# HGRN2 recurrence with a max-out feed-forward: five early steps of a hand-written order moved, and span 2's keys loaded ahead of its queries

## The chip, the cores and the metric

The kernel runs on one core of a Trainium2 chip. The metric is the device time of one launch in microseconds (us), lower is better. A core has TensorE (PE; its weight loads are listed apart as PEld), VectorE (DVE), ScalarE (ACT), GpSimd (POOL) and SyncE (SP, which here only issues transfers, its queue shown as SPq). Each engine works through its own list of instructions strictly in order and waits for others by semaphores; 16 DMA engines move data between HBM and the on-chip SBUF; matmul results lie in eight PSUM banks.

## The reference, cut to what matters

```python
# q, k, v, f_logit: (4, 8, 768, 48) = batch, heads, sequence, head size
f = 1.0 / (1.0 + np.exp(-f_logit))
for t in range(S):
    state = f[:, :, t, :, None] * state + np.einsum('bhd,bhe->bhde', k[:, :, t], v[:, :, t])
    y[:, :, t] = np.einsum('bhd,bhde->bhe', q[:, :, t], state)
x = y.transpose(0, 2, 1, 3).reshape(3072, 384)
return np.maximum(x @ w1, x @ w2) @ w_out          # w1, w2: 384 x 1024, w_out: 1024 x 384
```

## The kernel before

The 3072 tokens are cut into 12 spans of 256 tokens; span s belongs to batch s % 4, and the recurrence is carried from span s to span s + 4. Two neighbouring tokens share a partition (even and odd), so a span is 128 partitions; it is worked as two chunks of 64 partitions. Decays become products within a chunk: q and k are scaled by exponentials of summed log gates, the intra-chunk part is a masked matrix of q against k, and the state is added through further matmuls. The feed-forward uses max(a, b) = b + relu(a - b): the kernel forms wd = w1 - w2 and m2 = w2 @ w_out once, and each span then costs relu(x @ wd) @ w_out + x @ m2.

Nothing is scheduled by a compiler. One long string, ORDER, lists every step; a word is a step's letter, the span (or the quarter of a weight), an engine letter (a ScalarE, v and w VectorE, p GpSimd, s SyncE) and, after @, a PSUM bank or, for loads, an SBUF slot. The last loop of the kernel runs the words one by one, so the string is at the same time the order of each engine's instruction list. Of it, these words matter here:

| word | what it is | line |
|---|---|---|
| Lf, Lk, Lq, Lv | load gates, keys, queries, values of a span into one slot (SP's queue) | 115 |
| Wa, Wb, Wo | load halves of w1, w2, w_out into two slots each (SP's queue) | 126, 130 |
| E, F, G | gate = exp(-f), ell = ln(1 + gate), one = exp(-ell of the odd token) (ScalarE) | 192, 196, 200 |
| e | e = ell even + ell odd, what the sum over tokens is taken of | 203 |
| C | that sum, on TensorE | 207, 210 |
| X, Z | exponentials of the sum, for keys (inv) and for queries and decays (dec) (ScalarE) | 217, 222 |
| i, j | multiply the even half of the keys by `one`; of the queries by (1 + gate) | 226, 230 |
| K, Q | the scaled keys and queries in bf16 | 237, 240 |
| V | values to bf16 | 104 |
| t, u | transposes of keys and of queries on TensorE | 257 |
| U | both transposes copied out of PSUM (trs) | 104 |
| A, m | queries against keys on TensorE; that, masked, to SBUF (at_m) | 274, 282 |
| S, z, y | a span's output: its first state part on TensorE, a one-column VectorE copy from it (look), the rest | 314, 330, 342 |
| D, n | the sum that updates the state; its addition on VectorE | 358, 375 or 377 |
| Y | the span's output to bf16 (xT) | 104 |
| d, r | x @ wd on TensorE; relu to SBUF (gT) | 398, 407 or 409 |
| o, oz, b | the output products; their copy to SBUF | 424, 104 |
| ws | a quarter of wd = w1 - w2 | 485 |
| wc, wt, wx | w2 to bf16, transposed on TensorE, copied out of PSUM (ob) | 104, 459, 104 |
| wo | a quarter of w_out to bf16 | 104 |
| wm, wn | m2 on TensorE; its copy to SBUF (m) | 475, 104 |

Steps copy through one helper, so many operations carry its line, 104. Keys and queries are loaded as float32 into slots that the weights used before; i and j write in place over them, and K and Q read them after that. TensorE's list around the change runs, in words: the d of spans 0 and 1, wm0, wm2, C2, wm1, C3, o0.0, oz0.0, t2, D2, u2, o1.0, A2.0, A2.1, o0.1, S2 (with D3 mixed in), D3, t3, y2, u3, o1.1.

The step that the change reorders around:

```python
def step_i(s, e):
    even = loaded[s]["k"][:, :, 0, :]
    engines[e].tensor_mul(even, even, one[s])

def step_j(s, e):
    even = loaded[s]["q"][:, :, 0, :]
    engines[e].scalar_tensor_tensor(out=even, in0=gate[s][:, :, 1, :], scalar=1.0, in1=even,
                                    op0=ALU.add, op1=ALU.mult)
```

Of the kernel before, what the change touches and what calls it, by code (L numbers as in the profile page):

```python
# [21 lines left out]
t0@0 Lv1s@13 u0@0 E1 D0@2 Wb0s U0v@0 F1 n0.0v A0.0@0 e1p G1 Wa0s n0.1v S0@4 Wb1s A0.1@2 z0 Wa1s i1p  # L22
m0.0v@0 C1@6 Wo0s Z1 Wo1s j1v X1 V1a K1v Lf2s@16 Q1v t1@6 wc0a m0.1v@2 u1@6 D1@0 wc1a U1v@6 y0 n1.0v
n1.1v A1.0@6 Y0a@4 N1.1w S1@2 ws0p m1.0v@6 A1.1@0 wt0@4 z1 m1.1v@0 wt1@5 Lf3s@17 ws1p wx0a@4 d0.0@6
wx1a@5 y1 wc3v d0.1@7 wc2v Y1v@2 wt2@5 r0.0a@6 wt3@4 ws2v d1.0@2 Lq2s@0 ws3p d1.1@3 wx2v@5 d1.2@6
Lk2s@1 wx3v@4 d0.2@0 r1.0v@2 wo2a wo3p d0.3@1 Lv2s@2 wo0a wo1p d1.3@7 r0.1v@0 E2 wm0@2 Lk3s@8 F2
r1.1v@6 wm2@3 E3 e2p Lq3s@16 G2 C2@6 F3 j2v wm1@7 Lv3s@17 wn2a@3 e3v X2 C3@3 Z2 i2v o0.0@0 wn0a@2
Lf4s@9 K2v wn1a@7 V2a Q2v oz0.0@0 t2@6 Lf5s@1 X3 D2@4 N0.1v G3 u2@6 n2.0v o1.0@2 b0.0a@0 i3p U2v@6
Lk4s@0 n2.1v j3v A2.0@6 Lq5s@2 b1.0a@2 A2.1@4 K3p o0.1@0 m2.0v@6 Z3 V3a Lv4s@10 m2.1v@4 S2@6 E4 D3@2
z2 Q3v Lq4s@8 t3@4 F4 y2 u3@4 G4 e4p Lk5s@16 o1.1@1 b0.1a@0 U3v@4 Y2a@6 i4p E5 n3.0v Lf7s@9 n3.1v  # L30
C4@0 b1.1v@1 d2.0@4 X4 Z4 A3.0@2 K4p Lv5s@1 A3.1@6 F5 d2.1@5 m3.0v@2 G5 d2.2@0 Lk7s@17 r2.0a@4
m3.1v@6 e5p S3@2 d2.3@1 V4a z3 C5@4 j4v Lq7s@0 y3 X5 Q4v Z5 t4@6 Y3a@2 D4@4 r2.1v@0 N2.1p Lf6s@10
u4@6 i5p d3.0@2 n4.0v d3.2@0 U4v@6 Lf8s@8 d3.1@3 j5v d3.3@1 r3.0a@2 N4.0w Lk6s@11 N3.1p o2.0@6 n4.1v
# [514 lines left out]
```

## Time and profile before

| | |
|---|---|
| time, median of 3 runs | 139.65 us (139.54 to 139.70) |
| the profiled execution: own time, span from first to last instruction | 139.23 us, 137.4 us |
| busy: PE, DVE, ACT, POOL | 120.9, 104.0, 81.2, 43.9 us |
| granted TensorE clock | 1.00 |
| traffic | 28.68 MB, loads of spans in pieces of 384 bytes, DMA engines busy nine tenths or more up to about 93 us |

The page of the profile gives each engine's busy time, then the waits, then a chain: from the last instruction back to what released it, and so on to the start. A line of the timeline is start, duration, engine, line, operation, output <- input, how many instructions are merged, and in brackets the idle time just before it and what ended that. Because the lists are in order, an engine's instruction can be late by its own inputs or by whatever stands ahead of it.

### The profile page before, as it was taken

What the parts mean: (1) busy time and instruction counts of PE and PEld (TensorE: products, weight loads), DVE (VectorE), ACT (ScalarE), POOL (GpSimd) and SP (SyncE); (2) the same over time, 40 slices, a digit from 0 to 9 for tenths busy, and PEclk for the clock granted to TensorE, in tenths of its full rate; (3) what the DMA queues carried; (4) which work ended last, traced back from release to release, by engine and by line L of the source; (5) the groups of instructions that cost most, each with busy time, mean ns of one, the idle gap of its engine ahead of it and who ended that gap; (6) DMA issues with size and microseconds to landing.
All of it is one profiled execution on the core that took longest, in us unless ns stands there. A gap on an engine that the chain in (4) does not pass through costs nothing.

```text
span 137.4 us, 5777 instructions
## 1 busy us (share of the span) xinstructions
PE 120.9 (88%) x2575; PEld 89.9 (65%) x2575; DVE 104.0 (76%) x165; ACT 81.2 (59%) x120; POOL 43.9 (32%) x53
## 2 busy tenths in 40 slices
PE   0047397999998999999999999999999999999991
PEld 0035285775656688666787667886578876778671
DVE  5778999995897799888969995988988369620321
ACT  3646564269945982888499454988817570226210
POOL 7704109542160786217104320002804912000000
PEclk9999999999999999999999999999999999999999
DMA  4999999999999999999999999994104001103033
GB/s 108 270 261 261 367 389 378 347 257 262 268 263 244 246 272 252 241 256 293 277 235 319 336 278 255 328 284 99 46 0 176 1 7 62 34 28 119 0 114 115
DMA packets 55193, 28.68 MB, mean 209 GB/s; under 512 B 50304, under 2 KB 52736, under 8 KB 55168
## 3 DMA queue, kind: packets, MB, share of 16 engines
q1 hardware_dynamic: 55024, 28.25, 78.6%
q8 instruction: 20, 0.33, 1.0%
q10 hardware_dynamic: 144, 0.07, 0.2%
q14 instruction: 5, 0.04, 0.1%
HBM read 23.59 MB, written 4.72 MB: 206 GB/s over the span
## 4 chain that ended last, share of the span: by engine, by line
PE 72%; DMA 13%; DVE 5%; SPq 3%; ACT 3%; issue 1%
PE banks L424 30%; PE banks L398 20%; DMA slots<-in_moe_w_out_dram 10%; PE banks L342 5%; PE banks L257 4%; PE banks L274 4%; PE banks L475 3%; PE banks L314 3%; DMA slots<-in_f_logit_dram 3%; SPq L126 2%; PE banks L358 2%; PE banks L207 2%; DVE at_m L282 2%; ACT wo L104 1%; DVE slots L230 1%
## 5 line engine op out<-in xcount | busy, mean ns | idle before, releaser
L424 PE MATMUL banks<-wo,gT 128*128 128x384 bf16 (+2 forms) x200 | 35.3, 320 | 0.0
L398 PE MATMUL banks<-xT,wd 128*128 128x256 bf16 x288 | 34.1, 273 | 1.2 <-POOL wd L485 0.9
L398 PEld LDWEIGHTS <-wd 128*128 128x128 bf16 x288 | 27.0, 98 | 5.3 <-POOL wd L485 1.0
L282 DVE TENSOR_TENSOR at_m<-banks,mask 128x1024 bf16<-128x1024 f32 x24 | 28.8, 1217 | 2.2 <-PE banks L274 2.0
L424 PEld LDWEIGHTS <-gT 128*128 128x128 bf16 x200 | 19.2, 98 | 11.9
L407 ACT ACTIVATE gT<-banks 128x1024 bf16<-128x1024 f32 x15 | 15.2, 1019 | 11.4 <-PE banks L398 10.6
L203 POOL TENSOR_TENSOR e<-ell 128x384 bf16<-128x384 f32 x9 | 9.1, 1019 | 26.9 <-ACT ell L196 21.4
L424 PE MATMUL banks<-m,xT 128*128 128x384 bf16 (+2 forms) x75 | 15.9, 321 | 0.0
L409 DVE TENSOR_SCALAR gT<-banks 128x1024 bf16<-128x1024 f32 x9 | 10.9, 1219 | 6.3 <-PE banks L398 6.3
L104 DVE COPY trs<-banks 128x2048 bf16<-128x2048 bf16 x10 | 12.0, 1220 | 4.6 <-PE banks L257 4.6
L104 ACT COPY ob<-banks 128x384 f32<-128x384 f32 (+2 forms) x15 | 7.5, 506 | 13.2 <-PE banks L424 12.6
L104 ACT CAST xT<-banks 128x768 bf16<-128x768 f32 x10 | 8.0, 800 | 9.0 <-PE banks L342 8.9
L104 DVE COPY ob<-banks 128x384 f32<-128x384 f32 (+2 forms) x14 | 7.2, 541 | 7.5 <-PE banks L424 5.6
L192 ACT ACTIVATE gate<-slots 128x768 f32<-128x768 f32 x12 | 10.0, 837 | 4.4 <-DMA slots<-in_f_logit_dram 4.4
L342 PE MATMUL banks<-at_m,vb 64*64 64x128 bf16 x576 | 11.5, 224 | 0.0
L380 POOL TENSOR_TENSOR st<-tmp_s,dec 128x192 bf16<-128x192 f32 x8 | 4.1, 510 | 20.7 <-PE banks L274 12.9
L274 PE MATMUL banks<-trs 48*64 48x128 bf16 x384 | 9.9, 230 | 0.8 <-DVE trs L104 0.8
L226 POOL TENSOR_TENSOR slots<-slots,one 128x384 f32<-128x384 f32 x7 | 8.1, 1160 | 7.5 <-ACT one L200 6.9
L196 ACT ACTIVATE ell<-gate 128x768 f32<-128x768 f32 x12 | 10.1, 843 | 0.5
L207 PE MATMUL banks<-e,u_inc 128*128 128x384 bf16 x12 | 4.2, 353 | 6.9 <-DVE e L203 6.7
L342 PEld LDWEIGHTS <-vb 64*64 64x64 bf16 x576 | 10.0, 111 | 0.0
L240 DVE TENSOR_TENSOR qp<-slots,dec 128x768 bf16<-128x768 f32 x10 | 9.4, 951 | 0.1
(64 smaller groups left out, 173.2 us busy)
## 6 DMA issues: line engine op xcount, KB each, us to landing
slots<-in_f_logit_dram SPq DMA_DIRECT2D x12, 384.0 KB, 6.3
slots<-in_k_dram SPq DMA_DIRECT2D x12, 384.0 KB, 6.0
slots<-in_q_dram SPq DMA_DIRECT2D x12, 384.0 KB, 6.2
slots<-in_v_dram SPq DMA_DIRECT2D x12, 384.0 KB, 6.0
slots<-in_moe_w_dram SPq DMA_DIRECT2D x4, 768.0 KB, 9.2
out_dram<-ob SPq DMA_DIRECT2D x7, 384.0 KB, 5.4
out_dram<-ob SPq DMA_DIRECT2D x9, 192.0 KB, 1.9
slots<-in_moe_w_out_dram SPq DMA_DIRECT2D x2, 768.0 KB, 13.5
```

The costliest lines, as they stand in the source:

```text
L104: (nc.scalar.copy if e == "a" else engines[e].tensor_copy)(out, in_)
L192: nc.scalar.activation(flat(gate[s]), flat(loaded[s]["f"]), AF.Exp, bias=0.0, scale=-1.0)
L196: nc.scalar.activation(flat(ell[s]), flat(gate[s]), AF.Ln, bias=1.0, scale=1.0)
L203: engines[e].tensor_add(pad("e", s)[:, :, 0:D], ell[s][:, :, 0, :], ell[s][:, :, 1, :])
L240: engines[e].tensor_mul(pad("qp", s)[:, :, :, 0:D], by_parity(loaded[s]["q"]), both(dec[s][:, 0:HD].rearrange("p (h d) -> p h d", h=H)))
L274: nc.tensor.matmul(out=ps[h * HC:(h + 1) * HC, j % 2, par, :], lhsT=t[rows, h, 0, j, par, :], rhs=t[rows, h, 1, j].rearrange("p a t -> p ( ...
L282: nc.vector.tensor_mul(at[s][:, jj].rearrange("p r j a t -> p (r j) (a t)"), banks[:, b:b + 2, :].rearrange("p r (j x) -> p (r j) x", j=2) ...
L342: nc.tensor.matmul(out=ys[s][h][cols, kt, :], lhsT=window(vb[rows, par], head, off), rhs=m[rows, head // 4, head % 2, head // 2 % 2, par, ...
L398: nc.tensor.matmul(out=ps[:, f, :], lhsT=wd[:, kt, ff * C:(ff + 1) * C], rhs=x_flat(g)[:, kt, :], start=(kt == 0), stop=(kt == KT - 1))
L407: nc.scalar.activation(dst, src, AF.Relu)
L409: nc.vector.tensor_relu(dst, src)
L424: nc.tensor.matmul(out=ps, lhsT=x, rhs=w, start=(n == 0), stop=(n == KT + FG - 1))
```

## The change

Only the string ORDER differs. On the engines this means:

- Y1 goes from VectorE to ScalarE, ws3 and e2 from GpSimd to VectorE, wo1 from GpSimd to ScalarE, and wo0 with it stands ahead of wo2 on ScalarE.
- j3 (queries of span 3, VectorE) stands behind the two m2 and z2 rather than ahead of them.
- On SP's queue the keys of span 2 are loaded ahead of its queries, and the two loads swap slots 0 and 1.
- On VectorE i2 (keys of span 2) comes ahead of j2 (queries of span 2), and both ahead of e3. The list was j2, e3, i2, K2, Q2; it becomes e2, i2, j2, e3, K2, Q2.

TensorE's list is unchanged.

```diff
-wx1a@5 y1 wc3v d0.1@7 wc2v Y1v@2 wt2@5 r0.0a@6 wt3@4 ws2v d1.0@2 Lq2s@0 ws3p d1.1@3 wx2v@5 d1.2@6
-Lk2s@1 wx3v@4 d0.2@0 r1.0v@2 wo2a wo3p d0.3@1 Lv2s@2 wo0a wo1p d1.3@7 r0.1v@0 E2 wm0@2 Lk3s@8 F2
-r1.1v@6 wm2@3 E3 e2p Lq3s@16 G2 C2@6 F3 j2v wm1@7 Lv3s@17 wn2a@3 e3v X2 C3@3 Z2 i2v o0.0@0 wn0a@2
+wx1a@5 y1 wc3v d0.1@7 wc2v Y1a@2 wt2@5 r0.0a@6 wt3@4 ws2v d1.0@2 Lk2s@0 ws3v d1.1@3 wx2v@5 d1.2@6
+Lq2s@1 wx3v@4 d0.2@0 r1.0v@2 wo0a wo1a wo2a wo3p d0.3@1 Lv2s@2 d1.3@7 r0.1v@0 E2 wm0@2 Lk3s@8 F2
+r1.1v@6 wm2@3 E3 e2v Lq3s@16 G2 C2@6 F3 i2v j2v wm1@7 Lv3s@17 wn2a@3 e3v X2 C3@3 Z2 o0.0@0 wn0a@2
...
-Lk4s@0 n2.1v j3v A2.0@6 Lq5s@2 b1.0a@2 A2.1@4 K3p o0.1@0 m2.0v@6 Z3 V3a Lv4s@10 m2.1v@4 S2@6 E4 D3@2
-z2 Q3v Lq4s@8 t3@4 F4 y2 u3@4 G4 e4p Lk5s@16 o1.1@1 b0.1a@0 U3v@4 Y2a@6 i4p E5 n3.0v Lf7s@9 n3.1v
+Lk4s@0 n2.1v A2.0@6 Lq5s@2 b1.0a@2 A2.1@4 K3p o0.1@0 m2.0v@6 Z3 V3a Lv4s@10 m2.1v@4 S2@6 E4 D3@2 z2
+j3v Q3v Lq4s@8 t3@4 F4 y2 u3@4 G4 e4p Lk5s@16 o1.1@1 b0.1a@0 U3v@4 Y2a@6 i4p E5 n3.0v Lf7s@9 n3.1v
```

## The prediction

> **What bounds the kernel now.** I read the page first (busy times), then the chain of waits in order of time, then the timelines of VectorE, TensorE and GpSimd around the change, and last the table of transfers. The page:
>
> ```profile
> PE 120.9 (88%) x2575; PEld 89.9 (65%) x2575; DVE 104.0 (76%) x165; ACT 81.2 (59%) x120; POOL 43.9 (32%) x53
> DMA  4999999999999999999999999994104001103033
> ```
>
> TensorE does most, but an average does not say where it waits. The chain does:
>
> ```profile
> 14.37 14.11 DMA slots<-in_moe_w_out_dram
> 28.47 0.02 issue
> 28.50 1.57 ACT wo L104 x2
> 30.07 0.04 issue
> 30.11 2.76 PE banks L475 x16
> ...
> 37.35 0.35 DVE st L377
> 37.70 0.04 issue
> 37.74 1.23 DVE trs L104
> 38.97 0.26 DVE tmp_s L375
> 39.23 1.35 DVE slots L230
> 40.58 2.28 DVE at_m L282 x2
> 42.86 0.04 issue
> 42.90 0.41 PE banks L257 x16
> ```
>
> Up to 30.11 the second half of w_out bounds; up to 37.3 TensorE; then VectorE, with j3 (L230) in the middle, until t3 at 42.90. From there to 134.67 the chain holds TensorE alone, without a gap. So whatever t3 or u3, the next steps that wait for VectorE, win or lose arrives at the end undiminished; nothing can be lost or won later unless a new wait appears.
>
> VectorE's list, where the change swaps i2 and j2 (lines 226 and 230):
>
> ```profile
> 32.93 0.56 DVE L230 SCALAR_TENSOR_TENSOR slots<-gate,slots 128x384 f32<-128x384 f32 x1 [1.35 <-DMA slots<-in_k_dram]
> 33.60 0.56 DVE L203 TENSOR_TENSOR e<-ell 128x384 bf16<-128x384 f32 x1
> 34.15 0.56 DVE L226 TENSOR_TENSOR slots<-slots,one 128x384 f32<-128x384 f32 x1
> ```
>
> j2 sat idle for a load. The two loads, issued at 24.60 (q2) and 28.22 (k2):
>
> ```profile
> slots<-in_q_dram SPq DMA_DIRECT2D x1, 384.0 KB, 8.1
> slots<-in_k_dram SPq DMA_DIRECT2D x1, 384.0 KB, 5.9
> ```
>
> So q2 landed at 24.60 + 8.1 = 32.7 and k2 at 28.22 + 5.9 = 34.1. The bracket names keys, but j2 needs q2 and ran while k2 was under way; both transfers are on one queue, 1.4 us apart, and DMA is full. e3 stands behind j2 and ahead of i2, so today it needs only the first of the two loads. TensorE took C3, which needs e3, without a pause, at 34.37.
>
> **The change, part by part.**
>
> *Ahead of C3: gains.* ws3 leaves GpSimd. There ws3 (24.36 to 26.17) ran beside VectorE's ws2 (24.87, 2.12 us long; a product of the same size takes 0.95 at line 240). On VectorE the two run one after the other from about 24.3, when the last half of w1 is in: 24.3 + 2 x 0.95 = 26.2. d1.2, which waited 0.31 for ws2, then starts at the end of d1.1, 26.73. Y1 on ScalarE costs 0.80 in a stretch where ScalarE idles (2.31 ahead of 24.79) and frees 0.95 of VectorE. wo0 and wo1 go ahead of wo2 on ScalarE: their half landed at 13.48 + 12.8 = 26.3, so they run (2 x 0.8) before the other half lands at 28.47, and m2's product loses its 0.28 wait. Together TensorE reaches C2 and wm1 0.31 + 0.28 = 0.59 earlier; e2 on VectorE, after F2 (30.84 + 0.84), ends at 32.25 and costs C2 at most 0.1. TensorE would be ready for C3 at 34.37 - 0.59 + 0.08 = 33.86. Without ScalarE's spare time, wo1 would cost E2 0.8; with f2 landing at 29.9 the cover holds.
>
> *At C3: a loss.* The queue's places keep their times: I take 32.7 for k2 and 34.1 for q2, because f2, f3, q2 and k2 land 1.3 to 1.5 us apart with full engines and nothing ahead of them in SP's queue changes. SP does not gain or lose either: slots 0 and 1 are free at 23.87 (ws1), before it gets there. VectorE: i2 waits for G2 (32.32 + 0.51), runs 32.9 to 33.5; j2 waits for q2, 34.17 to 34.73; **e3 now stands behind both**, 34.72 to 35.28; C3 at 35.33 instead of 34.37, a shift of 0.96, with TensorE idle for 35.33 - 33.86 = 1.47. The start after a landing is the free term: before, j2 started 0.2 after it with two semaphore instructions ahead; now one wait is left, 0.04 taken, so the shift is 0.85 to 1.12. The 0.59 won ahead is swallowed by this wait. K2 (35.3 to 36.25) and Q2 (to 37.1) end before t2 and u2 come, at 36.52 + 0.96 and 37.22 + 0.96. Values of span 2 land at 35.5 as before. The load into slot 1 (f5) waits for Q2, 37.1 instead of 36.85; its landing is 7 us after issue with the queue full, so I cost it at nothing; a gap in the queue would cost 0.3 and would first show at F5.
>
> *From C3 to t3: a part comes back.* u2 38.18, o1.0 38.52, A2.0 39.45 + 0.96 = 40.41; U2 is done by then (38.64 + 1.23 = 39.87). With j3 gone, m2.0 starts at 40.41 + 0.47 (the distance of A3.0 and m3.0, 47.35 to 47.82) = 40.88 and the second m ends at 43.23. TensorE reaches t3 at 42.52 + 0.96 = 43.48 and finds it free: t3's wait of 0.38 is gone. Net at t3: 0.96 - 0.38 = +0.58.
>
> *At u3: a part goes again.* j3 is now between z2 and Q3, and Q3 releases u3:
>
> ```profile
> 42.77 0.14 DVE L330 COPY look<-banks 128x1 f32<-128x1 f32 x1
> 42.84 0.94 DVE L240 TENSOR_TENSOR qp<-slots,dec 128x768 bf16<-128x768 f32 x1
> ...
> 44.20 0.41 PE L257 MATMUL banks<-ident,qp 64*128 64x64 bf16 x16
> ```
>
> z2 needs S2. S2 starts at 41.92 + 0.96 = 42.88, is done 0.40 later (41.92 to 42.27, and 0.05); then z2 to j3 0.07, j3 0.56 (GpSimd idle beside it; 1.44 before, when K3 ran there), 0.10 as between j4 and Q4, Q3 0.94, 0.05 to TensorE: 2.12 in all, u3 at 45.00. TensorE's own path from S2 to u3 is 0.60 + 1.30 = 1.90. So u3 waits 0.22 (0 to 0.35, as S2's end is modelled).
>
> *Sum:* 0.96 - 0.38 + 0.22 = +0.80 (0.45 to 1.10). The profiled execution goes from 139.23 to 140.03, its span from 137.4 to 138.2. The runs' median stands 0.42 above that execution; 139.65 + 0.80 = 140.45.
>
> **Rivals.** About 0.2% (0.28 us) is what a measurement of this kernel can tell from no change.
>
> 1. *VectorE's order bounds, not the load: no slower.* If q2 lands by 33.45, i2, j2 and e3 run back to back from G2: e3 ends at 32.87 + 3 x 0.56 = 34.55, C3 at 34.60, shift 0.23; u3 0.23 - 0.38 + 0.22 = +0.07, that is 139.72. It decides below a landing of 33.6, where the sum falls under 0.28. Against it: the second load of this pair landed at 34.1. Chance 0.07.
> 2. *The loads run ahead: faster.* If the whole queue gained over 1.1 us (f3, k2, q2), e3 would no longer bind; with 1.4, C3 at 33.9, shift -0.47, u3 -0.63: 139.0. For it: the engines moved 374 GB/s in the stretch of the weights against 252 from 28.47 on. Against it: their pieces differ, and those do not change. Chance 0.05.
> 3. *Q3 meets e4 on GpSimd.* Q3 is due at 43.99, e4 starts at 44.40, when F4 is done, by a load that does not move:
>
> ```profile
> 39.15 1.44 DVE L230 SCALAR_TENSOR_TENSOR slots<-gate,slots 128x384 f32<-128x384 f32 x1
> ...
> 44.40 1.00 POOL L203 TENSOR_TENSOR e<-ell 128x384 bf16<-128x384 f32 x1 [4.23 <-ACT ell L196]
> ```
>
> j3 beside K3 (38.36 to 40.17) ended 0.42 after K3, ws2 0.82 after ws3: a VectorE product that starts second stands until GpSimd is through. If Q3 came 0.41 later than I have it, it would end at 45.40 + 0.82, u3 at 46.27, +2.07: 141.7. In its time it is first, and GpSimd waits instead, as i4 (51.18, 1.81 long) beside Q4. [...] Chance 0.05.
> 4. *TensorE goes slow in the idle 1.47.* Sixteen transposes took 0.61 at 16.69 and 0.41 at 36.52, so the array was slower early on, though the granted clock is shown as 1.00 throughout; the longest pause since is 0.88, ahead of 22.15, and the six products behind it took 0.83 like those at 23.92. A pause of 1.47 has no row. If it brought back the early rate for the 4.6 us from 15.83 to 20.43, that would cost up to 4.6 x (1 - 0.41 / 0.61) = 1.5 more: 141.95. [...] Chance 0.03.
>
> **How the numbers follow.** The forecast has 0.80; its own range, 140.1 to 140.75, with 0.1 for the spread of runs is 140.0 to 140.85. With rival 1 (139.72) taken in at the lower end and 0.1 for Q3 a little late at the upper, 139.7 to 140.95 leaves out rivals 2, 3 and 4, 0.13. Slower: 0.80 + 0.05 + 0.03 = 0.88; same 0.07; faster 0.05.
>
> **What would show it.** Right: VectorE runs i2 at about 32.9, j2 idles until 34.1 to 34.2, e3 ends near 35.3, TensorE has a gap of about 1.5 before line 207 there; the chain holds the q2 load, j2 and e3; no wait before t3, a short one before u3 released by Q3 (line 240); then TensorE without gaps, everything 0.8 later. Wrong: C3 without a gap, q2 landing before 33.6, or a gap before u3 over 1 us.

## The result, and the profile after

The changed kernel takes 141.50 us (median of 4 runs, 141.42 to 141.65) against 139.68 (139.54 to 140.08) for the kernel before: ratio 1.0128, 95% interval 1.0101 to 1.0155. Slower, as forecast, but 1.8 us slower and not 0.8, and outside the range given. A second measurement of the same kernel (changed_again below) gave 141.18 against 140.00, ratio 1.0099 (1.0065 to 1.0132). The profiled execution of the kernel before took 139.23, 0.45 less than the median of its runs here, so shifts that are read against that profile come out about that much larger than the 1.8 between the medians.

The page of the changed kernel, the counterpart of the first two lines shown of before:

```profile
PE 121.1 (87%) x2575; PEld 89.9 (64%) x2575; DVE 104.1 (75%) x166; ACT 83.0 (59%) x122; POOL 40.4 (29%) x50
DMA  4999999999999999999999699994104001013033
```

As before, busy shares tell nothing: TensorE does the same work in a longer span. The chain of waits in order of time (start, duration, what), from the load of the queries on:

```profile
28.36 5.99 DMA slots<-in_q_dram
34.34 0.02 issue
34.37 0.04 DVE slots L230
34.40 0.44 issue
34.84 0.56 DVE e L203
35.41 0.05 issue
35.45 0.34 PE banks L207
...
43.41 0.16 DVE look L330
43.57 0.48 DVE slots L230
...
44.14 1.64 DVE qp L240
45.78 0.05 issue
45.82 0.41 PE banks L257 x16
...
53.62 0.36 PE banks L358 x29
53.97 0.66 issue
54.63 0.21 PE banks L358 x3
...
129.79 7.19 PE banks L424 x55
```

The first group is the loss that was forecast: the load of q2, then j2 (L230), then e3 (L203), then C3. The second is z2 (L330), j3 and a Q3 (L240) of 1.64, where 0.94 was forecast, then u3. The third is a pause of TensorE inside D4. Everything after that keeps its lateness to the last 55 matmuls: 129.79, against 127.48 before. VectorE's list at the first group, TensorE's C3 and u3 with the idle time before each, and the two loads, issued at 24.74 (keys) and 28.36 (queries):

```profile
33.21 0.56 DVE L226 TENSOR_TENSOR slots<-slots,one 128x384 f32<-128x384 f32 x1 [0.87 <-DMA slots<-in_q_dram]
34.37 0.56 DVE L230 SCALAR_TENSOR_TENSOR slots<-gate,slots 128x384 f32<-128x384 f32 x1 [0.60 <-DMA slots<-in_q_dram]
34.84 0.55 DVE L203 TENSOR_TENSOR e<-ell 128x384 bf16<-128x384 f32 x1
```

```profile
35.45 0.34 PE L207 MATMUL banks<-e,u_inc 128*128 128x384 bf16 x1 [1.33 <-DVE e L203]
...
45.82 0.41 PE L257 MATMUL banks<-ident,qp 64*128 64x64 bf16 x16 [0.91 <-DVE qp L240]
```

```profile
slots<-in_k_dram SPq DMA_DIRECT2D x1, 384.0 KB, 8.3
slots<-in_q_dram SPq DMA_DIRECT2D x1, 384.0 KB, 6.0
```

Keys landed at 24.74 + 8.3 = 33.0, queries at 28.36 + 6.0 = 34.4. The bracket of i2 names the queries, but i2 reads keys and started 0.2 after they were in; queries were still 1.2 away. So i2 and j2 each wait for their own load, and e3, which needs neither, stands behind them.

Where the lateness arises, by the starts of four steps on TensorE and of the last 55 matmuls (shifts against the first profile of before in brackets):

| | C3 | t3 | u3 | u4 | last 55 |
|---|---|---|---|---|---|
| before | 34.37 | 42.90 | 44.20 | 52.47 | 127.48 |
| forecast | 35.33 (+0.96) | 43.48 (+0.58) | 45.00 (+0.80) | | (+0.80) |
| changed | 35.45 (+1.08) | 43.55 (+0.65) | 45.82 (+1.62) | 54.78 (+2.31) | 129.79 (+2.31) |
| changed_again | 35.39 (+1.02) | 43.48 (+0.58) | 45.76 (+1.56) | 54.36 (+1.89) | 129.49 (+2.01) |

Up to t3 the forecast holds within 0.12. Then two steps cost what it did not have: u3, and u4. GpSimd's list of the changed kernel shows who else was at work there (e4; the step ahead of i5, and i5); under it VectorE's products (Q3; j4 and Q4):

```profile
43.95 1.00 POOL L203 TENSOR_TENSOR e<-ell 128x384 bf16<-128x384 f32 x1 [3.58 <-ACT ell L196]
...
51.76 0.52 POOL L380 TENSOR_TENSOR st<-tmp_s,dec 128x192 bf16<-128x192 f32 x1
52.23 1.33 POOL L226 TENSOR_TENSOR slots<-slots,one 128x384 f32<-128x384 f32 x1
```

```profile
44.14 1.63 DVE L240 TENSOR_TENSOR qp<-slots,dec 128x768 bf16<-128x768 f32 x1
...
51.78 0.92 DVE L230 SCALAR_TENSOR_TENSOR slots<-gate,slots 128x384 f32<-128x384 f32 x1
52.80 1.57 DVE L240 TENSOR_TENSOR qp<-slots,dec 128x768 bf16<-128x768 f32 x1
```

Q3 started 0.19 behind e4 and ended 0.82 after it: rival 3 of the prediction. Q4 started at 52.80, in the middle of i5 (52.23 to 53.56), and ended 0.81 after it: the same collision a second time. Neither shows as a wait; it lies inside the product's own duration, 1.63 and 1.57 instead of 0.95.

### The profile page after: what moved, and what is told of

It reads as the page before. It is cut to its first block, busy times and chain, and to the rows that moved or that the text cites. A ratio compares the mean times of both kernels' runs of the same rounds, so it can differ in the third digit from the quotient of the medians.

```text
span 139.7 us, 5773 instructions
## 1 busy us (share of the span) xinstructions
PE 121.1 (87%) x2575; PEld 89.9 (64%) x2575; DVE 104.1 (75%) x166; ACT 83.0 (59%) x122; POOL 40.4 (29%) x50
## 4 chain that ended last, share of the span: by engine, by line
PE 71%; DVE 9%; issue 6%; DMA 4%; POOL 4%; SPq 3%; ACT 1%; POOLq 0%; DVEq 0%
PE banks L424 32%; PE banks L398 19%; PE banks L342 4%; DMA slots<-in_q_dram 4%; PE banks L257 4%; PE banks L274 4%; PE banks L314 3%; SPq L115 3%; DVE at_m L282 2%; PE banks L358 2%; DVE qp L240 2%; PE banks L207 2%; DVE w2b L104 1%; POOL st L165 1%; POOL vb L165 1%
## 5 line engine op out<-in xcount | busy, mean ns | idle before, releaser
L203 POOL TENSOR_TENSOR e<-ell 128x384 bf16<-128x384 f32 x8 | 8.1, 1024 | 26.7 <-ACT ell L196 19.1
L104 ACT CAST xT<-banks 128x768 bf16<-128x768 f32 x11 | 8.8, 799 | 10.5 <-PE banks L342 10.4
L240 DVE TENSOR_TENSOR qp<-slots,dec 128x768 bf16<-128x768 f32 x10 | 10.7, 1079 | 0.2
L380 POOL TENSOR_TENSOR st<-tmp_s,dec 128x192 bf16<-128x192 f32 x8 | 4.8, 602 | 20.5 <-PE banks L274 12.9
```

The costliest lines, as they stand in the source:

```text
L104: (nc.scalar.copy if e == "a" else engines[e].tensor_copy)(out, in_)
L203: engines[e].tensor_add(pad("e", s)[:, :, 0:D], ell[s][:, :, 0, :], ell[s][:, :, 1, :])
L240: engines[e].tensor_mul(pad("qp", s)[:, :, :, 0:D], by_parity(loaded[s]["q"]), both(dec[s][:, 0:HD].rearrange("p (h d) -> p h d", h=H)))
```

## Experiments

The theory under test: (a) the loss begins at C3 since e3 stands on VectorE behind a load that it doesn't need; (b) this delay moves Q3 and Q4 into products of GpSimd, e4 and i5, and each such meeting costs again. The experiments have two rivals of their own, numbered anew. Rival 1: the moved steps cost it, above all j3's place. Rival 2: the swapped loads themselves.

| kernel | us (median) | ratio to before, 95% interval | C3 | t3 | u3 | u4 | last 55 |
|---|---|---|---|---|---|---|---|
| e3_between | 139.01 | 0.9957 (0.9935 to 0.9978) | 34.21 | 42.30 | 43.91 | 52.28 | 127.33 |
| j3_early | 140.29 | 1.0035 (1.0011 to 1.0059) | 35.53 | 43.63 | 44.92 | 53.52 | 128.65 |
| moves_only | 139.05 | 0.9963 (0.9941 to 0.9986) | 34.26 | 42.36 | 43.97 | 52.06 | 127.08 |
| swap_only | 140.26 | 1.0041 (1.0022 to 1.0060) | 35.21 | 43.30 | 44.60 | 52.69 | 128.60 |
| queries_first | 141.76 | 1.0150 (1.0109 to 1.0191) | 35.83 | 43.92 | 46.20 | 54.81 | 129.99 |
| e4_vector | 140.39 | 1.0055 (1.0026 to 1.0084) | 35.13 | 43.22 | 44.83 | 53.43 | 128.56 |
| e4_i5_vector | 140.26 | 1.0053 (1.0032 to 1.0074) | 35.30 | 43.40 | 45.01 | 53.11 | 128.26 |
| e3_first | 138.80 | 0.9951 (0.9928 to 0.9974) | 34.45 | 42.53 | 43.95 | 52.06 | 127.17 |
| e3_between_j3_early | 139.44 | 0.9964 (0.9941 to 0.9986) | 34.44 | 42.53 | 43.94 | 53.26 | 128.26 |

The positions are those of one profiled execution each. The times of one kernel spread by well over 1 us (before: 138.98 to 140.41 in 35 runs; e3_first: 138.46 to 140.06 in 12), so the ratios with their intervals decide, and the profiles' positions say where.

**e3_between: e3 between i2 and j2.**

```diff
-... F3 i2v j2v wm1@7 Lv3s@17 wn2a@3 e3v X2 C3@3 Z2 o0.0@0 wn0a@2
+... F3 i2v wm1@7 Lv3s@17 wn2a@3 e3v X2 C3@3 Z2 j2v o0.0@0 wn0a@2
```

> The changed kernel with one step elsewhere on VectorE: e3 between i2 and j2 (e2, i2, e3, j2, K2, Q2); the load order stays keys first. Theory (the loss begins at C3, because e3 stands behind a load it doesn't need, and two collisions of VectorE with GpSimd over SBUF follow from the delay): C3 at 34.3 instead of 35.45, t3 near 42.5 instead of 43.55, Q3 starts near 43.0, ahead of e4, and takes 0.95 instead of 1.63; u3 near 44.0 instead of 45.82; Q4 ahead of i5; time 139.2 to 139.6. Rival 1 (the moved steps cost it, j3 behind z2 above all): within 0.3 of the changed kernel, 141.2 to 141.8. Rival 2 (the swapped loads themselves hold up what follows): the same, 141.2 to 141.8.

Measured: 139.01, a little below the range expected. VectorE's list now runs e3 in j2's waiting time, and C3 waits 0.16 in place of 1.33:

```profile
32.98 0.56 DVE L226 TENSOR_TENSOR slots<-slots,one 128x384 f32<-128x384 f32 x1 [0.70 <-DMA slots<-in_q_dram]
33.59 0.56 DVE L203 TENSOR_TENSOR e<-ell 128x384 bf16<-128x384 f32 x1
34.13 0.56 DVE L230 SCALAR_TENSOR_TENSOR slots<-gate,slots 128x384 f32<-128x384 f32 x1
```

One step moved within one engine's list turns a loss of 1.3% into a gain of 0.4% over the kernel before, with the keys still loaded first. Q3 took 0.96, Q4 0.96. Both rivals fall for the bulk of the loss.

**queries_first: the loads as before, VectorE still i2, j2, e3.**

```diff
-... Lk2s@0 ws3v d1.1@3 wx2v@5 d1.2@6 Lq2s@1 ...
+... Lq2s@0 ws3v d1.1@3 wx2v@5 d1.2@6 Lk2s@1 ...
```

> The changed kernel with the two loads back in their old order (q2 first) but VectorE still in the order i2, j2, e3. Theory (e3 stands behind whichever load lands last): i2 waits for keys that land at 34.1 and j2 follows, so e3 ends 0.55 later than in the changed kernel, C3 near 35.9; Q3 near 44.6, behind e4; no better than the changed kernel, 141.4 to 142.2. Rival 2 (the load order itself is what costs): with the old order the loss goes, 139.0 to 139.8.

Measured: 141.76, at or above the changed kernel. Now i2 idles for the keys and e3 ends later still:

```profile
34.28 0.56 DVE L226 TENSOR_TENSOR slots<-slots,one 128x384 f32<-128x384 f32 x1 [1.79 <-DMA slots<-in_k_dram]
34.75 0.55 DVE L230 SCALAR_TENSOR_TENSOR slots<-gate,slots 128x384 f32<-128x384 f32 x1
35.22 0.55 DVE L203 TENSOR_TENSOR e<-ell 128x384 bf16<-128x384 f32 x1
```

With e3_between this settles (a): it is not which load comes first but that e3 stands behind the last of the two.

**moves_only and swap_only: each half of the change alone.** moves_only has the changed kernel's five moves with loads and VectorE order of span 2 as before; swap_only is the kernel before with these words:

```diff
-Lq2s@0 ... Lk2s@1 ... F3 j2v wm1@7 Lv3s@17 wn2a@3 e3v X2 C3@3 Z2 i2v
+Lk2s@0 ... Lq2s@1 ... F3 i2v j2v wm1@7 Lv3s@17 wn2a@3 e3v X2 C3@3 Z2
```

> The five steps moved as in the change, but loads and products of span 2 as before (q2 loaded first, VectorE j2, e3, i2). Theory: C3 near 34.3, u3 near 44.0, Q3 ahead of e4; 139.2 to 139.6, at or a little below the kernel before. Rival 1 (the moved steps cost): most of the loss is here, 140.8 to 141.5. Rival 2 (the load order): as the kernel before, 139.65.

> The kernel before with only the keys of span 2 loaded first and i2, j2 ahead of e3. Theory: C3 at 35.4, t3 near 43.6, Q3 (directly behind z2) ahead of e4 or in a near tie with it, u3 0.7 later than before, Q4 behind i5 for another 0.6; 140.3 to 141.0. Rival 1 (the moved steps cost): 139.6. Rival 2 (the load order): nearly all of the loss, 141.4.

Measured: 139.05 and 140.26. The moves alone gain 0.4%; the swap alone loses 0.4%. Rival 1, the moves by themselves, is out. But neither half alone makes the 1.3%: in moves_only Q3 started at 42.95 and in swap_only at 43.25, ahead of e4 (43.65 and 43.77) in both. Only where C3 is late and j3 stands between z2 and Q3 does Q3 fall behind e4, so j3's new place is part of the cause, together with the swap. In swap_only C3 came at 35.21, but u3 was 0.40 later and not 0.7, and Q4 did not meet i5 (0.96 long); in its place TensorE paused 0.58 at 70.05 for nothing that the profile shows. The time came out just below what was expected, with another second half.

**j3_early: j3 back ahead of the two m2.**

```diff
-... n2.1v A2.0@6 ... D3@2 z2 j3v Q3v ...
+... n2.1v j3v A2.0@6 ... D3@2 z2 Q3v ...
```

> The changed kernel with j3 back ahead of the two m2 on VectorE. Theory: C3 stays at 35.4 and t3 at 43.5 (VectorE idles 0.69 ahead of m2.0, j3 fits there); Q3 starts near 43.5, ahead of e4 at 43.95, takes 0.95, and u3 comes without a wait near 44.9 instead of 45.82; Q4 still falls behind i5; 0.9 less than the changed kernel, 140.6. Rival 1 (j3's place costs it by itself, about its own 0.56): 140.9. Rival 2 (the load order): unchanged, 141.5.

Measured: 140.29. t3 stays (43.63), and Q3, 0.5 earlier, is ahead of e4; it is e4 that waits now (1.36 long). VectorE, GpSimd and TensorE there:

```profile
43.57 0.96 DVE L240 TENSOR_TENSOR qp<-slots,dec 128x768 bf16<-128x768 f32 x1
```

```profile
44.03 1.36 POOL L203 TENSOR_TENSOR e<-ell 128x384 bf16<-128x384 f32 x1 [3.61 <-ACT ell L196]
```

```profile
44.92 0.41 PE L257 MATMUL banks<-ident,qp 64*128 64x64 bf16 x16
```

u3 has no wait. Q4 still met i5 (1.57). Against the changed kernel this one move is worth about 1 us. The wait of 0.24 that e3_between shows ahead of u3 is j3's own part of that; the larger part is the collision.

**e4_vector and e4_i5_vector: GpSimd's product taken away.** The first puts e4 on VectorE behind Q3, the second i5 behind Q4 as well.

```diff
-... G4 e4p ...       ... u4@6 i5p ...
+... G4 e4v ...       ... u4@6 i5v ...
```

> The changed kernel with e4 on VectorE, directly behind Q3, in place of GpSimd. [...]

> The changed kernel with e4 and i5 on VectorE, behind Q3 and behind Q4. Theory: both products take 0.95, only the wait for e3 at C3 is left, which is +0.65 at t3 and 0.2 more at u3 against the kernel before: 140.1 to 140.6. Rival (the pause of 0.66 in D4 of the changed kernel belongs to TensorE's own issue and not to Q4): 0.4 more than that, 140.6 to 140.9, and a pause without a releaser is seen again.

Measured: 140.39, where 140.7 to 140.9 was expected, and 140.26. In the first Q3 is 0.96, where 1.6 would have meant that its own data held it; in the second Q4 is 1.08. Q3 in e4_vector:

```profile
43.81 0.96 DVE L240 TENSOR_TENSOR qp<-slots,dec 128x768 bf16<-128x768 f32 x1
```

TensorE's u4 in the one and the other:

```profile
53.43 0.41 PE L257 MATMUL banks<-ident,qp 64*128 64x64 bf16 x16 [0.42 <-DVE qp L240]
```

```profile
53.11 0.41 PE L257 MATMUL banks<-ident,qp 64*128 64x64 bf16 x16
```

From t4 to u4 it is 1.20 and 0.72: the meeting with i5 costs 0.48 in the profile. The medians differ by 0.13 only, less than their intervals, so by time alone the second collision is not resolved; the first is (141.2 to 141.5 down to 140.39), though e4_vector's interval, up to 1.0084, overlaps that of changed_again, from 1.0065; j3_early's, up to 1.0059, does not. That leaves (b) shown for Q3 by time and profile, for Q4 by profile.

**changed_again and before_again, before_third: both kernels once more, without an edit.**

> The changed kernel once more, to see which of its losses come back. Theory (Q3 due at 44.0 to 44.1 and e4 due at 43.4 to 44.0 in nearly every run, since the gates of span 4 land at 41.4 to 41.8 in seven of eight profiles and at 42.46 only in the first profile of the kernel before): Q3 behind e4 again, about 1.6 long, u3 waiting 0.7 to 1.2; Q4 behind i5 again, about 1.57; 141.2 to 141.7. Rival (the first look was unlucky): Q3 0.95, time 140.4 to 140.8. The pause of 0.66 in D4, with no releaser, is left open by the theory: with it 141.5, without it 0.35 less.

> The kernel before once more, for a second look at its two groups of times (about 139.1 and 139.8). Theory A (a near tie of Q4 and i5, which started within 0.01 of each other in the first look): in a run of the slower group Q4 takes about 1.6 and u4 comes 0.5 later. Theory B (TensorE pauses about 0.6 for instructions): Q4 takes 0.95 and the chain shows one pause without a releaser. If the run falls in the faster group, neither is seen.

> The kernel before, a third look: whether TensorE's slow phase ends near 20 (first look: the six products at 22.15 took 0.83) or near 26 (second look: 1.46 there, C3 0.64 later and t3 without its wait). Theory: both occur, and the time is 139.0 to 139.3 with the early end and 139.4 to 140.0 with the late one. Rival: the times' two groups have another cause, and the slow phase ends early in a run of over 139.5 or late in one under 139.2.

changed_again: 141.18, Q3 1.63 behind e4 at 43.88, Q4 1.58 behind i5, no pause in D4: the two collisions came in both profiles of this kernel, the pause in one. Of the gates' landings that its expectation speaks of, the count over all fourteen profiles is: ten between 41.4 and 41.8, four between 42.2 and 42.8. The kernel before took 139.42 and 139.72 in these profiled executions, against 139.23 in the one that the prediction was made on. In before_again TensorE was slow until about 26 (see below), C3 came 0.64 later, and t3's wait of 0.38 was gone, so that only 0.20 was left at the end. before_third goes against the theory stated for it: 139.72 with the slow phase over early (the six products at 22.10 took 0.83). There 0.40 of the lateness arises behind u4: VectorE waited 0.67 for a load of queries and 0.36 for an output store, so its copy of output rows (ob) started at 67.90, where the first profile has 66.61, and TensorE's transposes at 72.45 waited 0.23 for the queries scaled behind that copy. That is one execution; what parts the two groups of the kernel before in general is left open.

**e3_first and e3_between_j3_early: versions meant to beat both.**

```diff
-... G2 C2@6 F3 i2v j2v wm1@7 Lv3s@17 wn2a@3 e3v X2 C3@3 Z2 ...   ... D3@2 z2 j3v Q3v
+... F3 C2@6 G2 wm1@7 Lv3s@17 wn2a@3 e3v X2 C3@3 Z2 i2v j2v ...   ... D3@2 j3v z2 Q3v
```

e3_between_j3_early is e3_between with the second hunk alone.

> A version meant to beat both: the changed kernel with F3 ahead of G2 on ScalarE, VectorE in the order e2, e3, i2, j2, K2, Q2, and j3 behind the two m2 but ahead of z2. Theory: e3 waits for no load at all, ends near 33.7, C3 near 33.95 without a pause (34.2 in e3_between), Q2 ends near 36.7, in time for u2; Q3 near 42.5, u3 without the 0.24 wait of e3_between; 0.3 to 0.5 below e3_between: 138.5 to 138.8. Rival (what e3 waits for was not the only thing; the pair's second load holds K2 and Q2 now): C3 early, but t2 or u2 waits for K2 or Q2, and the time is that of e3_between, 139.0.

> e3_between with j3 behind the two m2 but ahead of z2 (there j3 need not wait for S2). Theory: Q3 starts 0.1 to 0.2 earlier and u3 loses its wait of 0.24; 138.8 to 138.9. Rival (the wait is Q3's own data, or TensorE is slower elsewhere): 139.0 as e3_between.

e3_first: 138.80, below the kernel before by 0.5% and, within the intervals, no different from e3_between. C3 did not come at 33.95: at 34.45 it waited for the copy of m2 out of its bank on ScalarE (wn2, behind F3 and G2, which ended at 34.40), so e3, which ended at 34.22, was no longer last. u3's wait is gone in both (1.42 and 1.41 from t3, 1.61 in e3_between), but the second shows no gain in time (139.44, where 138.8 to 138.9 was expected), and its profiled execution fell on a pause of 1.00.

## Why the prediction was wrong

- **C3, +0.96: right.** +1.08 and +1.02. The gains ahead of it (no wait for ws2 or for w_out) came too, and they were swallowed: TensorE stood idle 1.33 ahead of C3, where 1.47 was forecast. C2 waited 0.43 for e2 on VectorE, where at most 0.1 was forecast; that was swallowed as well. The queries landed at 34.34 rather than 34.1.
- **t3, its wait gone, net +0.58: right.** +0.65 and +0.58.
- **u3, forecast to wait 0.22: this step failed, it waited 0.91.** The failing term is Q3's 0.94: it was 1.63, behind e4. What the step did count, j3 behind z2, was right: in e4_i5_vector, with e4 and i5 off GpSimd, u3 waits 0.24 and the last 55 matmuls start 0.78 later than before, so the sum of +0.80 is what the mechanisms in it are worth.
- **Rival 3 had the mechanism, but a chance of 0.05.** The premise that failed is "e4 starts at 44.40, when F4 is done, by a load that does not move". With the same place in the queue, the gates of span 4 landed at 42.4 (35.34 + 7.1) in the one profile at hand and at 41.7 (35.57 + 6.1) in the changed kernel. e4 started at 43.95, 0.45 earlier than forecast, and Q3 at 44.14, 0.15 later; the margin was 0.41. It was taken as one when the end it was measured to varies by over a microsecond between runs (41.4 to 42.8). And in the changed kernel the landing no longer set e4 at all. ScalarE's list there (V3, then E4), and E4 before:

```profile
41.42 0.83 ACT L104 CAST vb<-slots 128x768 bf16<-128x768 f32 x1
42.14 0.85 ACT L192 ACTIVATE gate<-slots 128x768 f32<-128x768 f32 x1
```

```profile
42.54 0.84 ACT L192 ACTIVATE gate<-slots 128x768 f32<-128x768 f32 x1 [1.38 <-DMA slots<-in_f_logit_dram]
```

  E4 ran right behind V3, with its gates in for 0.4. That list and VectorE's both follow TensorE, so Q3 stood the same 0.19 behind e4 in all three profiles that have this order (the changed kernel twice, and queries_first, 0.4 later). The time of rival 3, 141.7, is near the measured one by luck: it had u3 at +2.07 and nothing after it, where u3 came at +1.62 and a second loss followed at u4.
- **Q4 behind i5 was not in the prediction.** In the profile of before, VectorE's Q4 and GpSimd's i5 stood at

```profile
51.17 0.96 DVE L240 TENSOR_TENSOR qp<-slots,dec 128x768 bf16<-128x768 f32 x1
```

```profile
51.18 1.81 POOL L226 TENSOR_TENSOR slots<-slots,one 128x384 f32<-128x384 f32 x1 [0.53 <-DVE slots L230]
```

  with Q4 ahead by a hundredth (by 0.03 in before_again and 0.33 in before_third). i5 had been held until its keys came in at 51.0. With VectorE 1.6 later those keys are long there (51.0 again), i5 follows at once behind the step ahead of it, and Q4, which starts 0.10 after j4, loses. The line was cited (there as i4) for its 1.81 as proof that GpSimd waits; that the order hung on 0.01 was not read from it.
- **Rivals 1, 2 and 4 did not occur.** After the idle 1.33 the eleven matmuls behind C3 took 1.81, as before. So an idle of 1.33 did not bring the slow phase back, nor did the 1.57 ahead of C3 in queries_first, where those eleven took 1.81 too.
- **"TensorE without gaps" after u3: wrong in one place, u4.** In changed_again u4 waited 0.42 for Q4, and the lateness grew by 0.45 from u3 to the last 55. In the first profile it grew by 0.69: Q4 was done at 54.37, but the pause in D4 held TensorE until 54.63, so there the pause ended last.

## What to carry to other kernels

In an in-order list, put a step that does not need a load ahead of the steps that wait for it; here moving one 0.56 us addition past a wait decided between 1.3% slower and 0.4% faster. When a step is forecast to come later, check each VectorE product of the kind of Q3 and Q4 (L240) on its new place against GpSimd's products: here a meeting did not show as a wait but as a product of 1.6 instead of 0.95, and the order hung on as little as 0.01 us. Here an end that depended on a landing was known from one profile only to about a microsecond (41.4 to 42.8 for one load over fourteen profiles), so a margin smaller than that deserves a large chance, not a small one.

## What the runs showed of the hardware

- The VectorE products Q3 and Q4, started while GpSimd's product ran, ended 0.82 after e4 and 0.81 after i5; alone they take 0.95. A GpSimd product that started second was longer too: e4 took 1.36 in j3_early, 1.00 alone. The tiles that these products read and write all lie in SBUF; at what the two engines meet there no run shows.
- TensorE's slow phase at the start ends at different times: the six products at the start of d0.0, in the first and in the second profile of before, both with a granted clock shown as 1.00:

```profile
22.15 0.83 PE L398 MATMUL banks<-xT,wd 128*128 128x256 bf16 x6 [0.88 <-POOL wd L485]
```

```profile
22.20 1.46 PE L398 MATMUL banks<-xT,wd 128*128 128x256 bf16 x6
```

  So the end of the slow phase varies between runs: transposes that took 0.84 at 20.43 in the first profile took 1.46 at 20.63 in the second, whose slow phase ended near 26 (six products at 25.33 took 1.08, transposes at 26.25 took 0.83), over 5 us later. What ends it no run shows.
- In three profiles TensorE paused for 0.58 to 1.00 with no releaser. The one in D4 stood behind the same matmul of the list in the changed kernel (0.66) and in e3_between_j3_early:

```profile
51.68 0.43 PE L358 MATMUL banks<-vb,kp 64*64 64x48 bf16 x29
53.11 0.21 PE L358 MATMUL banks<-vb,kp 64*64 64x48 bf16 x3 [1.00 <-issue]
```

  and the one in swap_only (0.58) exactly 384 matmuls further, that is 768 instructions with their weight loads. The page lists q8 as an instruction queue, with 20 transfers and 0.33 MB, that is 16 KB each. One of them began at 50.5 in e3_between_j3_early and one at 49.4 in e3_between, where the pause at the same matmul is 0.07; TensorE went on 2.6 behind the one and 2.7 behind the other. That TensorE waits for its own instructions there is the author's guess from these times, not tried, and why the transfer is late at times is open.
